# An attention and two-MLP kernel: v loaded in token order by five transfers, and loads planned by their size

## The chip, the cores and the metric

The kernel runs on one core of one Trainium2 chip. The metric is the device time of the kernel in microseconds (us); lower is better. The core has five engines with queues of their own: TensorE (PE) multiplies matrices, VectorE (DVE), ScalarE (ACT) and GpSimd (POOL) work on rows of data, and SyncE (SP) issues the transfers between device memory and on-chip memory. PEld is TensorE's loading of weights, which overlaps its matmuls.

## The reference

Three stages follow each other. Cut to what matters:

```python
def attn(q, k, v):                     # (4, 8, 576, 64) each: batch, head, token, dim
    q_lm = q.reshape(B, H, 32, 18, D).mean(axis=3)      # 32 landmarks of 18 tokens
    k_lm = k.reshape(B, H, 32, 18, D).mean(axis=3)
    A, Bm, C = sm(q, k_lm), sm(q_lm, k_lm), sm(q_lm, k) # softmax of scaled products
    Z = Bm.T / (norm1(Bm) * norminf(Bm) + 1e-6)
    for _ in range(6):
        Z = 2 * Z - Z @ Bm @ Z
    return A @ Z @ C @ v
x = attn(q, k, v) as (2304, 512)
xn = x / sqrt(mean(x * x) + 1e-6) * rms_g
x = (silu(xn @ w_gate) * (xn @ w_val)) @ w_out          # d_ff 1536
out = (s * relu(x @ w_in) ** 2 + b) @ w_out2            # d_ff 2048; s and b are scalars
```

The five weight matrices come as float64 and everything else too small to matter here; q, k and v are float32.

## The kernel before

The work runs in three stretches that overlap at their edges. First comes the attention of batch 0, which only one chain of small steps on DVE, ACT and PE can produce. Then comes the first MLP for batches 0 to 3, half a batch (288 tokens) at a time, in 48 units (a batch and one of 12 slices of d_ff); while it runs for batch b, the attention of batch b + 1 is worked in between. Last comes the second MLP, in five blocks of up to 512 tokens by 16 slices.

Weights are float64 in device memory. `narrow` loads a tile of 512 KB into a staging buffer (`stage`, three of them, and three more inside `xbuf` once the attention of batch 0 is done), and makes float32 of it with three passes on ACT (the lines that write `ca` and `cmag`; the third can go to DVE) and one on DVE (which writes `rawg` or `rawo`). In batch 0 each of 12 slices needs three such tiles (gate, val, out). `rawg` has three buffers of two tiles each. The float32 tiles are stored back to device memory (`keptg`, `kepto`), and later batches load them from there.

No loop fixes the order of instructions. Each piece of work is handed to a planner (`Scheduler`) as an operation with an engine, a cost in us, a key and the data that it reads and writes. The planner walks through a time of its own: it takes the engine that can start earliest, gives it the ready operation with the lowest key, and emits its instructions. So the costs decide the order in which each engine gets its instructions, and on the chip each engine keeps that order and waits wherever the data is late. For a transfer the cost is the time until its data is taken as landed, and SP counts as free again a fixed time before that:

```python
free[e] = end if e != "sp" else end - 2.0
...
at(("sp", 5.2 if fine else 3.9), -0.3 if b else 0, load_heads, w=[t])
...
op(("sp", 3.46), key - 12, load, w=[st])
```

Here `at` is how the attention of a batch hands over its work, `load_heads` loads one of q and k for half the heads (one transfer for batches 0 and 1, four for the `fine` batches 2 and 3), and `load` is that of a weight tile. Keys of an attention's operations follow from how much work hangs behind each (`by_path`); those of batch 0 lie between -60 and -6, and those of the first weight tiles near -20.

v of a batch is one buffer, token by partition: five groups of up to 128 tokens, each with eight heads of 64 numbers. Before, v is laid out by a token order in which tokens that are 18 apart stand beside each other, because the scores and their exponentials (`eC`) come out of TensorE in that order. That takes 18 transfers of 32 partitions each. The product of `eC` with v is `cv_mm`; it needs rows of both in one order.

Of the kernel before, what the change touches and what calls it, by code (L numbers as in the profile page):

```python
# [37 lines left out]
XC = 2.0  # L38
COLD1 = 6.5
GV = 8  # L40
W2_STEP = 4.2
TO_F, TO_R = 0.09, 0.11
HOLD, FETCH = 2.0, 4.0

# [46 lines left out]
class Scheduler:  # L91
# [67 lines left out]
    def run(self, warm):  # L159
        free = dict.fromkeys(self.engines, 0.0)  # L160
        cand = {e: [] for e in self.engines}
        for o in self.ops:
            if not o.n_deps:
                for e in o.alts:
                    cand[e].append(o)
        left = len(self.ops)
        mode = "f"
        steady = False
        while left:
            best, port = None, None  # L170
            for e, ops in cand.items():
                ready = [(t, o) for o in ops if (t := self.start_of(o, e)) is not None]
                if not ready:
                    continue
                at = max(free[e], min(t for t, _ in ready))
                if best is None or at < best[0]:
                    best = (at, e, ready)
                if e in ("dve", "pool"):
                    o = min((o for t, o in ready if t <= at + self.SOON), key=lambda o: o.key)
                    if e in o.pair and (port is None or o.key < port[3] and at < port[0] + self.WAIT):  # L180
                        port = (at, e, ready, o.key)
            if best[1] in ("dve", "pool") and port and port[1] != best[1] and port[0] < best[0] + self.WAIT:
                o = min((o for t, o in best[2] if t <= best[0] + self.SOON), key=lambda o: o.key)
                if best[1] in o.pair and port[3] < o.key:
                    best = port[:3]
            at, e, ready = best
            shift = {}
            if e == "pe" and steady:
                shift = {"f": HOLD if mode == "r" else -FETCH}
            can = sorted(((o.key + shift.get(o.mode, 0.0), t, o) for t, o in ready if t <= at + self.SOON), key=lambda x: x[:2])  # L190
            for _, t, o in can:
                end = max(at, t) + o.alts[e] + o.spare.get(e, 0.0)
                if all(
                    max(free[a], self.start_of(o, a)) + d + o.spare.get(a, 0.0) >= end
                    for a, d in o.alts.items() if a != e
                ):
                    break
            else:
                _, t, o = can[0]
                a = min(o.alts, key=lambda a: max(free[a], self.start_of(o, a)) + o.alts[a] + o.spare.get(a, 0.0))  # L200
                e, at = a, max(free[a], at)
                end = max(at, self.start_of(o, a)) + o.alts[a]
            if e == "pe":
                t = max(WARM0, free["pe"])
                while (t := t + WCOST * (2 if t < COLD1 else 1)) <= min(at, WARM1) - WARMS:
                    warm()
            at = max(at, self.start_of(o, e))
            if e == "pe" and o.mode:
                steady = steady or o.mode == "r"
                if steady and o.mode != mode:  # L210
                    at = max(at, free[e] + (TO_R if o.mode == "r" else TO_F))
                mode = o.mode
            end = at + o.alts[e] * (2 if e == "pe" and at < COLD1 else 1)
            for b, s in self.slots_for(o).items():
                b.slot = s
                s.held = True
                if b.ring.queue:
                    b.ring.queue.remove(b)
            o.fn(self.engines[e])
            free[e] = end if e != "sp" else end - 2.0  # L220
            if e in o.pair:
                self.ports = end
            for b in o.bufs:
                b.left -= 1
                b.end = max(b.end, end)
                if not b.left:
                    b.slot.held, b.slot.free = False, b.end
            for u in o.users:
                u.ready[e] = max(u.ready.get(e, 0.0), end)
                u.n_deps -= 1  # L230
                if not u.n_deps:
                    for a in u.alts:
                        cand[a].append(u)
            for a in o.alts:
                cand[a].remove(o)
            left -= 1
# [5 lines left out]

def t_dve2(n):
    return 0.07 + 0.00052 * n


def t_act(n):
# [16 lines left out]
def tile_nystrom_attention_two_mlps(  # L264
# [18 lines left out]
    M = 32  # L283
# [110 lines left out]
    def consts(_):  # L394
# [12 lines left out]
        out=ident, in_=ones, pattern=[[-1, 128]], compare_op=ALU.is_equal,  # L407
        fill=0.0, base=0, channel_multiplier=1), r=["const"], w=["ident"])

    def load_small(e):  # L410
        e.dma_start(out=gT, in_=rms_g.rearrange("(k p) -> p k", p=128))
        e.dma_start(out=s_sb, in_=s2.rearrange("(o k) -> o k", o=1).to_broadcast([128, 1]))
        e.dma_start(out=b_sb, in_=b2.rearrange("(o k) -> o k", o=1).to_broadcast([128, 1]))

    op(("sp", 3.3), -20, load_small, w=["small"]).after = 6.0


    xs, gw = {}, {}
# [7 lines left out]
    def attention(b, t0, t1):  # L426
# [41 lines left out]
        for nm, a in (("k", k), ("q", q)):  # L468
            for g in range(2):
                t = src[nm, g] = Buf(qk_r[nm, g])  # L470

                def load_heads(e, t=t, a=a, g=g):
                    if not fine:
                        e.dma_start(
                            out=t.t.rearrange("p (t d) -> p t d", d=D),
                            in_=a[b, 4 * g:4 * g + 4].rearrange("h (i t) d -> (h i) t d", t=SEG))
                        return
                    for h in range(4):
                        e.dma_start(
                            out=t.t[32 * h:32 * h + 32].rearrange("p (t d) -> p t d", d=D),  # L480
                            in_=a[b, 2 * h + g].rearrange("(i t) d -> i t d", t=SEG))

                at(("sp", 5.2 if fine else 3.9), -0.3 if b else 0, load_heads, w=[t])
        vs = Buf(v_r)

        def vt():
            return vs.t.rearrange("p (j h d) -> p j h d", j=5, h=H)

        def load_v(e):
            sv = v[b].rearrange("h (i n) d -> n i h d", n=SEG)  # L490
            for n in range(SEG):
                e.dma_start(out=vt()[32 * (n % 4):32 * (n % 4) + 32, n // 4], in_=sv[token(b, n)])

        at(("sp", 9.5), -0.25 if b else 0.01, load_v, w=[vs])


        def loaded(g, h):
# [201 lines left out]
        def c_side(g, p0):  # L699
# [5 lines left out]
            for hf in range(2):  # L705
# [3 lines left out]
                    out=cm.t[:, hf:hf + 1], in_=pC[hf].t[:, 0:HC], axis=AX, op=ALU.max),  # L709
                    r=[pC[hf]], w=[(cm, hf)])  # L710

            def c_max(e):
                e.tensor_reduce(out=cm.t[:, 2:3], in_=cm.t[:, 0:2], axis=AX, op=ALU.max)
                e.tensor_scalar(out=cm.t[:, 3:4], in0=cm.t[:, 2:3], scalar1=-scale, scalar2=None, op0=ALU.mult)
# [1 line left out]
            at(("dve", 0.32), p0 + 0.02, c_max, r=[(cm, 0), (cm, 1)], w=[(cm, 3)])  # L716
            for hf in range(2):
                at(("act", t_act(HC) + 0.19), p0 + 0.03, lambda e, hf=hf: e.activation(
                    out=eC.t[:, HC * hf:HC * hf + HC], in_=pC[hf].t[:, 0:HC], func=ACTF.Exp,
                    scale=scale, bias=cm.t[:, 3:4], accum_out=cs.t[:, hf:hf + 1]),  # L720
                    r=[pC[hf], (cm, 3)], w=[(eC, hf), (cs, hf)])

# [212 lines left out]
    def narrow(key, kind, f, part, dst, w, after=()):  # L935
# [22 lines left out]
            return x.rearrange("p (n t) -> p n t", t=2)[:, :, i]  # L958

        n_ops = len(S_.ops)  # L960
        op(("sp", 3.46), key - 12, load, w=[st])
        def low():
            x = staged().bitcast(U8)
            if rows:
# [23 lines left out]
    def first_weights(key, b, f):  # L988

        r = Buf(rg_r)  # L990
        if b == 0:
            for part in range(2):
                narrow(key + 2.6 * part, 1, f, part, lambda part=part: r.t[:, part], (r, part))
            kept[0, f] = dr.tile([128, 2, 512], F32, name=f"keptg{f}")
            op(("sp", 3.7), key + 9, lambda e: e.dma_start(out=kept[0, f], in_=r.t),
               r=[(r, 0), (r, 1)], w=[("kept", 0, f)])
        else:
            op(("sp", 3.7), key - 8, lambda e: e.dma_start(out=r.t, in_=kept[0, f]),
               r=[("kept", 0, f)], w=[(r, 0), (r, 1)])
        return r  # L1000

    def out_weights(key, b, hf, f):
        r = Buf(ro_r)
        if b == 0 and hf == 0:
            narrow(key, 1, f, 2, lambda: r.t, r)
            kept[1, f] = dr.tile([128, 512], F32, name=f"kepto{f}")
            op(("sp", 3.0), key + 6, lambda e: e.dma_start(out=kept[1, f], in_=r.t), r=[r], w=[("kept", 1, f)])
        else:
            op(("sp", 3.0), key - 8, lambda e: e.dma_start(out=r.t, in_=kept[1, f]), r=[("kept", 1, f)], w=[r])
        return r  # L1010

    def weights(key, ring, src, r):
# [132 lines left out]
    def second_mm(key, j, f, w, hs):  # L1145
# [15 lines left out]
        for c in range(nt):  # L1161
# [10 lines left out]
                        in_=o.t[32 * i:32 * i + 32, :])  # L1172

            if j < NB - 1:
                op(("sp", 4.2), key, lambda e, store=store: store(e, range(4)), r=[o])
                continue
            op(("sp", 3.1), key, lambda e, store=store: store(e, (0, 1)), r=[o])
            op(("act", 1.1), key, lambda e, store=store: store(e, (2, 3)), r=[o])

    LEAD, LEAD_O = 6, 5  # L1180
# [102 lines left out]
    for i in range(NB * F2):  # L1283
# [3 lines left out]
        if f == F2 - 4 and j + 1 < NB:  # L1287
# [12 lines left out]
            else e.tensor_tensor(out=r.t[:, 0:n], in0=r.t[:, 0:n], in1=r.t[:, 0:n], op=ALU.mult)), r=[r], w=[r])  # L1300
        op({"pool": 0.3 + 0.0018 * n, "dve": 0.18 + t_dve2(n)}, t, lambda e, r=r, h=h, n=n: e.tensor_scalar(
            out=h.t[:, 0:n], in0=r.t[:, 0:n], scalar1=s_sb, scalar2=b_sb, op0=ALU.mult, op1=ALU.add),
            r=[r, "small", "hidden"], w=[h], pair=True)
        hh, hl = Buf(hs_r[0]), Buf(hs_r[1])
        split(t + 3, lambda hh=hh, n=n: hh.t[:, 0:n], lambda hl=hl, n=n: hl.t[:, 0:n],
              lambda h=h, n=n: h.t[:, 0:n], [h], hh, hl, n)
# [47 lines left out]
```

## Time and profile before

| | |
|---|---|
| time, median of 3 runs | 874.73 us (874.48 to 875.18) |
| the profiled execution | 874.78 us, of which the span from first to last instruction is 873.1 us |
| PE, PEld, DVE, ACT, POOL busy | 97%, 82%, 78%, 54%, 14% of the span |
| moved by the DMA engines | 105.96 MB, 121 GB/s on the mean |
| mean granted TensorE clock | 0.993 of full speed |

The shares are means over stretches that are limited by different things, so they say little about one edit. Matmuls are pipelined and overlap in the record, so a busy PE is not a PE at its peak. The DMA share of a stretch is how busy the core's 16 DMA engines were on the mean; it can show slightly over 1.

### The profile page before, as it was taken

Reading aid. Unit: us, or ns where it says so; the run is one execution under the profiler, and the core shown is the slowest. Engines: PE = TensorE matmul, PEld = TensorE weight load, DVE = VectorE, ACT = ScalarE, POOL = GpSimd, SP = SyncE. Lnnn points to the kernel's source line nnn. Section 1 sums busy time; section 2 is a strip of 40 time slices with the busy share of each in tenths; the row PEclk is TensorE's granted clock in tenths of the full one; section 3 lists DMA queues with packets and bytes.
Section 4 is the critical chain, followed back from the end, with each engine's and each line's share of the span. In section 5 each row is a group of like instructions: output and inputs, shape, how many; then the busy total and the mean of one; then the engine's idle time right before and its main releaser. Section 6 shows DMA issues by size and latency. Waiting matters only on the chain.

```text
span 873.1 us, 16943 instructions
## 1 busy us (share of the span) xinstructions
PE 844.8 (97%) x6386; PEld 716.6 (82%) x6386; DVE 679.2 (78%) x1500; ACT 472.1 (54%) x961; POOL 119.7 (14%) x153
## 2 busy tenths in 40 slices
PE   8978999999999999999999999999999999999997
PEld 5666666998799988899999888888888888888896
DVE  6968787888899888999899766766676667666786
ACT  4869868455563355477997433433343334333453
POOL 0260035501870033201000000000000000000000
PEclk9989999999999999999999999999999999999999
DMA  7798897785535413478985000010000000000100
GB/s 223 214 342 274 294 301 222 230 253 169 140 114 177 127 69 97 132 234 272 307 264 169 1 1 1 22 27 1 1 24 25 1 1 25 23 1 1 37 13 24
DMA packets 72513, 105.96 MB, mean 121 GB/s; under 512 B 25584, under 2 KB 46064, under 8 KB 72432
## 3 DMA queue, kind: packets, MB, share of 16 engines
q1 hardware_dynamic: 72240, 104.62, 38.4%
q8 instruction: 50, 0.82, 0.4%
q10 hardware_dynamic: 192, 0.26, 0.1%
q14 instruction: 31, 0.25, 0.1%
HBM read 90.70 MB, written 14.16 MB: 120 GB/s over the span
## 4 chain that ended last, share of the span: by engine, by line
PE 76%; DVE 10%; ACT 5%; DMA 5%; issue 2%; POOL 1%; SPq 0%; DVEq 0%; ACTq 0%; POOLq 0%
PE bank L1033 23%; PE bank L1155 22%; PE bank L1129 12%; PE bank L1079 11%; PE bank L1052 2%; PE bank L676 1%; PE bank L556 1%; DMA region<-in_k_dram 1%; ACT ca L968 1%; DVE ul L1067 1%; ACT cmag L970 1%; DVE wl L931 1%; DMA kepto<-rawo 1%; PE bank L1317 1%; DVE hbuf L1098 1%
## 5 line engine op out<-in xcount | busy, mean ns | idle before, releaser
L1295 ACT ACTIVATE hbuf<-bank 128x512 f32<-128x512 f32 (+1 forms) x79 | 44.0, 557 | 144.4 <-PE bank L1033 144.0
L1033 PE MATMUL bank<-xh,ul 128*128 128x512 f32 (+1 forms) x320 | 117.7, 368 | 0.0
L1033 PE MATMUL bank<-xl,uh 128*128 128x512 f32 (+1 forms) x320 | 117.6, 368 | 0.0
L1033 PE MATMUL bank<-xh,uh 128*128 128x512 f32 (+1 forms) x320 | 117.6, 367 | 0.0
L1155 PE MATMUL bank<-wh,hh 128*128 128x512 f32 x288 | 112.4, 390 | 0.3 <-DVE hh L930 0.3
L1155 PE MATMUL bank<-wl,hh 128*128 128x512 f32 x288 | 112.3, 390 | 0.0
L1155 PE MATMUL bank<-wh,hl 128*128 128x512 f32 x288 | 112.0, 389 | 0.0
L1129 PE MATMUL bank<-hh,wh 128*128 128x288 f32 x336 | 102.4, 305 | 0.3 <-ACT xbuf L1139 0.3
L1129 PE MATMUL bank<-hh,wl 128*128 128x288 f32 x336 | 98.8, 294 | 0.0
L1129 PE MATMUL bank<-hl,wh 128*128 128x288 f32 x336 | 98.8, 294 | 0.0
L1079 PE MATMUL bank<-xh,uh 128*128 128x288 f32 x248 | 77.8, 314 | 6.1 <-DVE ul L1067 3.1
L931 DVE TENSOR_TENSOR hl<-hbuf,hh 128x512 fp32r<-128x512 f32 (+2 forms) x134 | 78.2, 584 | 3.3 <-ACT hh L929 0.9
L1079 PE MATMUL bank<-xh,ul 128*128 128x288 f32 x248 | 74.4, 300 | 1.1 <-DVE ul L1067 1.1
L1079 PE MATMUL bank<-xl,uh 128*128 128x288 f32 x248 | 74.1, 299 | 0.0
L1129 PEld LDWEIGHTS bank<-hh,wh 128*128 128x128 f32 x336 | 63.0, 188 | 10.2 <-issue 8.9
L1033 PEld LDWEIGHTS bank<-xh,uh 128*128 128x128 f32 x320 | 60.1, 188 | 11.2
L1033 PEld LDWEIGHTS bank<-xl,uh 128*128 128x128 f32 x320 | 60.1, 188 | 11.0
L1033 PEld LDWEIGHTS bank<-xh,ul 128*128 128x128 f32 x320 | 60.0, 188 | 10.1
L929 ACT ACTIVATE wh<-region 128x512 fp32r<-128x512 f32 x48 | 30.4, 633 | 67.1 <-PE bank L1155 67.1
L930 DVE CAST uh<-region 128x512 fp32r<-128x512 f32 x57 | 24.3, 426 | 54.2 <-PE bank L1033 54.2
L931 DVE TENSOR_TENSOR wl<-rawo,wh 128x512 fp32r<-128x512 f32 x79 | 60.1, 761 | 5.2 <-ACT wh L929 0.8
L1155 PEld LDWEIGHTS bank<-wh,hl 128*128 128x128 f32 x288 | 54.1, 188 | 11.5 <-DVE hl L931 0.2
(219 smaller groups left out, 1989.5 us busy)
## 6 DMA issues: line engine op xcount, KB each, us to landing
rawo<-kepto SPq DMA_DIRECT2D x84, 256.0 KB, 3.1
rawg<-keptg SPq DMA_DIRECT2D x36, 512.0 KB, 4.6
stage<-in_moe_w_out_dram SPq DMA_DIRECT2D x28, 512.0 KB, 4.7
stage<-in_moe_w_in_dram SPq DMA_DIRECT2D x16, 512.0 KB, 5.0
keptg<-rawg SPq DMA_DIRECT2D x12, 512.0 KB, 7.5
region<-in_v_dram SPq DMA_DIRECT2D x72, 64.0 KB, 2.7
stage<-in_moe_w_val_dram SPq DMA_DIRECT2D x8, 512.0 KB, 6.6
xbuf<-in_moe_w_gate_dram SPq DMA_DIRECT2D x7, 512.0 KB, 6.8
```

Source lines behind the costliest of these rows:

```text
L556: nc.tensor.transpose(pT.t[:, 128 * j:128 * j + 128], s3.t[:, c:c + 128], ident)
L676: nc.tensor.matmul(out=ps.t[:, 0:HC], lhsT=part(u, "bd")[:, 128 * e:128 * e + 128], rhs=part(y, "t").rearrange("p (t e i) -> p t e i", e=2 ...
L929: e.activation(out=hi(), in_=src(), func=ACTF.Copy) if e is nc.scalar
L930: else e.tensor_copy(out=hi(), in_=src())), r=r, w=[wh], pair=True)
L931: b = op({"dve": t_dve(n), "pool": t_pool(n)}, key, lambda e: e.tensor_tensor(out=lo(), in0=src(), in1=hi().bitcast(F32), op=ALU.subtract) ...
L968: op(("act", 0.08 + t_act(512)), key, lambda e: e.activation(out=wide(a.t), in_=word(1).bitcast(F32), func=ACTF.Copy, scale=2.0 ** -112), ...
L1033: nc.tensor.matmul(out=ps.t[:, 0:n], lhsT=w[a].t[:, ks], rhs=x[y].t[:, kd, 0:n], start=(kd == 0 and i == 0), stop=(kd == KD - 1 and i == 2))
L1052: nc.tensor.matmul(out=pU[g].t[m, 256 * j:256 * j + 256], lhsT=gw[b].t[p, m], rhs=r.t[p, :, 128 * k:128 * k + 128], start=True, stop=True)
L1079: nc.tensor.matmul(out=ps.t[:, 0:HC], lhsT=u[a].t[:, 256 * g + 128 * part:256 * g + 128 * part + 128], rhs=x[y].t.rearrange("p k n -> p (k ...
L1129: nc.tensor.matmul(out=A[c].t[:, 0:HC], lhsT=w[a].t[:, 128 * c:128 * c + 128], rhs=hs[y].t[:, 0:HC], start=(f == 0 and i == 0), stop=(f == ...
L1155: nc.tensor.matmul(out=A[c].t, lhsT=hs[a].t[:, s], rhs=w[y].t, start=(f == 0 and i == 0), stop=(f == F2 - 1 and i == 2))
L1295: e.activation(out=r.t[:, 0:n], in_=ps.t[:, 0:n], func=ACTF.Relu) if e is nc.scalar
```

## The change

Five edits are made together. (1) v is loaded in plain token order, by five transfers of up to 128 partitions (four of 256 KB and one of 128 KB) in place of 18 of 64 KB. (2) So that `eC` has the same order, the two exponential passes of a head group write their output through a rearranged view: each value goes 72 bytes from the one before it, where it went next to it. (3) The cost of a transfer is worked out from its size (`t_dma`), and SP is free 3.0 us before the data lands, not 2.0. (4) The RMS factor `gT` is loaded alone; (5) the scale and bias of the second MLP are loaded later, under a name of their own (`scale`). `V_SP` is not used.

```diff
+DMA_LAG = 3.0
+DMA_KB = 0.00272
...
-            free[e] = end if e != "sp" else end - 2.0
+            free[e] = end if e != "sp" else end - DMA_LAG
...
+def t_dma(kb, n=1):
+    return DMA_LAG + max(DMA_KB * kb, 0.45 * n)
...
+    op(("sp", t_dma(100)), -20, lambda e: e.dma_start(out=gT, in_=rms_g.rearrange("(k p) -> p k", p=128)),
+       w=["small"]).after = 6.0
+
     def load_small(e):
-        e.dma_start(out=gT, in_=rms_g.rearrange("(k p) -> p k", p=128))
         e.dma_start(out=s_sb, in_=s2.rearrange("(o k) -> o k", o=1).to_broadcast([128, 1]))
         e.dma_start(out=b_sb, in_=b2.rearrange("(o k) -> o k", o=1).to_broadcast([128, 1]))
 
-    op(("sp", 3.3), -20, load_small, w=["small"]).after = 6.0
+    op(("sp", t_dma(100, 2)), 200.0, load_small, w=["scale"]).after = 130.0
...
-                at(("sp", 5.2 if fine else 3.9), -0.3 if b else 0, load_heads, w=[t])
+                at(("sp", t_dma(600, 4 if fine else 1)), -0.3 if b else 0, load_heads, w=[t])
...
         def load_v(e):
-            sv = v[b].rearrange("h (i n) d -> n i h d", n=SEG)
-            for n in range(SEG):
-                e.dma_start(out=vt()[32 * (n % 4):32 * (n % 4) + 32, n // 4], in_=sv[token(b, n)])
-
-        at(("sp", 9.5), -0.25 if b else 0.01, load_v, w=[vs])
+            for j in range(5):
+                n = min(128, S - 128 * j)
+                e.dma_start(out=vt()[0:n, j], in_=v[b][:, 128 * j:128 * j + n].rearrange("h n d -> n h d"))
+
+        at(("sp", t_dma(1310, 5)), -0.25 if b else 0.01, load_v, w=[vs])
...
+            def in_order(hf):
+                x = eC.t[:, 0:S]
+                if fine:
+                    return x.rearrange("p (i n) -> p n i", i=M)[:, HB * hf:HB * hf + HB]
+                return x.rearrange("p (i t e) -> p e t i", i=M, e=2)[:, hf]
...
                 at(("act", t_act(HC) + 0.19), p0 + 0.03, lambda e, hf=hf: e.activation(
-                    out=eC.t[:, HC * hf:HC * hf + HC], in_=pC[hf].t[:, 0:HC], func=ACTF.Exp,
+                    out=in_order(hf), in_=pC[hf].t[:, 0:HC].rearrange("p (t i) -> p t i", i=M), func=ACTF.Exp,
...
-        op(("sp", 3.46), key - 12, load, w=[st])
+        op(("sp", t_dma(512)), key - 12, load, w=[st])
...
-            op(("sp", 3.7), key + 9, lambda e: e.dma_start(out=kept[0, f], in_=r.t),
+            op(("sp", t_dma(512)), key + 9, lambda e: e.dma_start(out=kept[0, f], in_=r.t),
...
-            op(("sp", 3.7), key - 8, lambda e: e.dma_start(out=r.t, in_=kept[0, f]),
+            op(("sp", t_dma(512)), key - 8, lambda e: e.dma_start(out=r.t, in_=kept[0, f]),
...
-            op(("sp", 3.0), key + 6, lambda e: e.dma_start(out=kept[1, f], in_=r.t), r=[r], w=[("kept", 1, f)])
+            op(("sp", t_dma(256)), key + 6, lambda e: e.dma_start(out=kept[1, f], in_=r.t), r=[r], w=[("kept", 1, f)])
         else:
-            op(("sp", 3.0), key - 8, lambda e: e.dma_start(out=r.t, in_=kept[1, f]), r=[("kept", 1, f)], w=[r])
+            op(("sp", t_dma(256)), key - 8, lambda e: e.dma_start(out=r.t, in_=kept[1, f]), r=[("kept", 1, f)], w=[r])
...
-                op(("sp", 4.2), key, lambda e, store=store: store(e, range(4)), r=[o])
+                op(("sp", t_dma(256, 4)), key, lambda e, store=store: store(e, range(4)), r=[o])
...
-            op(("sp", 3.1), key, lambda e, store=store: store(e, (0, 1)), r=[o])
+            op(("sp", t_dma(128, 2)), key, lambda e, store=store: store(e, (0, 1)), r=[o])
...
-            r=[r, "small", "hidden"], w=[h], pair=True)
+            r=[r, "scale", "hidden"], w=[h], pair=True)
```

## Rows read from the trace of the kernel before

**Rows 1.** Windows: busy us (instructions) by engine, clock, DMA share, GB/s.

```profile
0.00:8.00 8.00, 6.19 (x29) 4.34 (x30) 3.50 (x24) 2.95 (x5) 0.50 (x5) 1.00 0.75 271
...
10.00:16.00 6.00, 6.00 (x93) 4.13 (x91) 3.61 (x12) 3.74 (x10) 0.00 (x0) 1.00 0.59 120
...
36.00:44.00 8.00, 7.17 (x78) 5.18 (x79) 7.30 (x21) 7.14 (x17) 1.58 (x2) 1.00 0.46 92
44.00:60.00 16.00, 11.68 (x75) 9.42 (x73) 10.31 (x18) 9.45 (x21) 13.85 (x20) 0.79 0.98 329
60.00:150.00 90.00, 83.54 (x851) 60.31 (x849) 71.68 (x185) 76.06 (x154) 17.76 (x23) 1.00 0.87 284
150.00:482.00 332.00, 325.59 (x3154) 298.24 (x3154) 295.53 (x691) 203.34 (x446) 80.67 (x96) 1.00 0.58 182
482.00:860.00 378.00, 378.00 (x1750) 316.23 (x1749) 261.02 (x467) 150.85 (x267) 0.00 (x0) 1.00 0.05 12
```

**Rows 2.** Chain that ended last, in order of time: start us, us, what.

```profile
18.63 0.60 ACT region L718 x2
...
44.50 4.90 DMA stage<-in_moe_w_val_dram
...
54.16 2.96 PE bank L1079 x12
...
97.53 7.63 DMA kepto<-rawo
...
138.82 3.56 DMA rawg<-keptg
...
153.35 3.18 PE bank L1079 x24
```

**Rows 3.** Timeline of ACT, 16 to 50 us: start, us, instruction, idle before.

```profile
16.36 0.26 ACT L607 ACTIVATE region<-region 128x64 f32<-128x64 f32 x1 [1.83 <-DVE region L605]
18.63 0.50 ACT L718 ACTIVATE region<-bank,region 128x288 f32<-128x288 f32 x1 [1.46 <-DVE region L714]
...
21.21 0.67 ACT L968 ACTIVATE ca<-stage 128x512 f32<-128x512 f32 x1 [1.51 <-DMA stage<-in_moe_w_gate_dram]
...
36.24 0.78 ACT L978 ACTIVATE cmag<-stage 128x512 f16<-128x512 f32 x1
...
44.63 0.39 ACT L1096 ACTIVATE hbuf<-bank 128x288 f32<-128x288 f32 x1
49.42 0.67 ACT L968 ACTIVATE ca<-stage 128x512 f32<-128x512 f32 x1 [4.40 <-DMA stage<-in_moe_w_val_dram]
...
51.36 0.65 ACT L968 ACTIVATE ca<-stage 128x512 f32<-128x512 f32 x1
```

**Rows 4.** Timeline of SP's transfers, 0 to 60 us: start, us, issue, count.

```profile
2.77 13.24 SPq L492 DMA_DIRECT2D region<-in_v_dram  x18
16.06 1.11 SPq L951 DMA_DIRECT2D stage<-in_moe_w_gate_dram  x1
...
19.31 0.51 SPq L411 DMA_DIRECT2D gT<-in_moe_rms_g_dram  x1
...
29.14 15.27 SPq L492 DMA_DIRECT2D region<-in_v_dram  x18
44.50 0.40 SPq L951 DMA_DIRECT2D stage<-in_moe_w_val_dram  x1
```

**Rows 5.** Single lines: issues of v, narrowing's third and second pass, and L842.

```profile
L492 SPq DMA_DIRECT2D region<-in_v_dram x72: 311/449/1496, 2.8 to 229.1; - x72
...
L978 ACT ACTIVATE cmag<-stage x54: 767/792/811, 22.5 to 470.7; 128x512 f16<-128x512 f32 x54
...
L970 ACT ACTIVATE cmag<-stage x57: 643/667/727, 21.8 to 470.0; 128x512 int32<-128x512 uint8 x57
...
L842 DVE TENSOR_TENSOR gw<-bank,gT x4: 281/288/293, 37.2 to 355.5; 128x128 f32<-128x128 f32 x4
```

**Rows 6.** SP's own waits, 0 to 60 us: total us, times, longest.

```profile
SPq L492 <- DMA region<-in_q_dram: 6.8, 4, 2.1
```

More of the change, by code (lines that the diff above doesn't have):

```diff
@@ L40 @@
 GV = 8
+V_SP = 5.0
 W2_STEP = 4.2
+DMA_LAG = 3.0
+DMA_KB = 0.00272
 TO_F, TO_R = 0.09, 0.11
```

## The prediction

> **What bounds the kernel now.** I read the table of windows first, to see which stretch can give time. From 482 to 860 us PE is busy in every microsecond and the transfers stand nearly still, and from 150 to 482 us PE lacks only 6.4 us of 332 [rows 1]: nothing about loads is to be won there, and a shift of what comes before is passed on whole. Between 60 and 150 us ACT is busy 76.1 of 90 us and the DMA engines 87%: float64 weights are loaded and narrowed there, and the two share the limit. The soft place is earlier. From 36 to 44 us the DMA engines are 46% busy at 92 GB/s, from 10 to 16 us 59% at 120 GB/s, although the stretches after each are short of weights [rows 1].
>
> The timeline of SP says why. v of batch 0 takes SP from 2.77 to 16.01 us, 18 issues, and the first weight tile is issued at 16.06. v of batch 1 takes it from 29.14 to 44.41, and the next weight tile (`w_val`, the sixth) is issued at 44.50 [rows 4]. SP does one thing at a time, so whatever stands behind v waits; part of it is that v's issues wait themselves for older transfers to land (6.8 us behind loads of q, in four waits) [rows 6].
>
> The timeline of ACT says what that costs. It is done at 45.02 (44.63 + 0.39) and starts the sixth tile at 49.42, 4.40 us idle until that load has landed [rows 3]. The chain of waits runs through the same load: 4.90 us from 44.50, then the narrowing, then 12 matmuls at 54.16 [rows 2]. The other chain links ahead of 44 us are attention of batch 0, on DVE, ACT and PE in turn, not loads; after 150 us they are matmuls.
>
> **The change, part by part.**
>
> *v by five transfers.* An issue of v takes 0.31 to 1.50 us, 0.45 in the middle [rows 5]. The trace has none of 256 KB with eight short runs per partition; five of them take SP 1.6 us if each costs the least and 7.5 if each costs the most. I take 2.7, five times 0.45 and one issue more for the gaps between them. Second train: 29.14 + 7.5 = 36.6 even at the dear end. The staging buffer that the sixth tile needs is the third tile's, whose last pass ends at 36.24 + 0.78 = 37.02 [rows 3]. So at either end of the bounds SP is free before the buffer is; the load goes out at about 37.0 and lands at about 37.0 + 4.9 = 41.9 [rows 2], before ACT is done with its attention work at 45.02. The whole wait goes: **-4.4 us**. What is late next is ACT itself: the sixth tile can also be narrowed in the gaps before 45. A tile occupies it 51.36 - 49.42 = 1.94 us [rows 3]. The three `rawg` buffers hold six tiles, so no more than this one gains: 0 to 1.94, and I take half, **-1.0**.
>
> First train: on the chip it should end near 5.5 us instead of 16.0 and free SP some 10 us earlier, but v's bytes must still pass. From 10 to 16 us the DMA engines moved 120 GB/s at a share of 0.59 [rows 1], so 203 GB/s at a full one; 1.18 MB of v take 5.8 us, behind q and k, of whose 2.36 MB 2.17 are through at 8 us (271 GB/s); the tile's own 0.52 MB take 1.6 us at the 329 GB/s of 44 to 60 us. So it lands at about 8.7 + 5.8 + 1.6, 16 to 17 us, where it was waited for until 21.21 [rows 3]. Up to 44 us the attention chain decides, so this alone gives nothing; it is what makes room for the sixth tile above. Later trains free SP too, but under a busy PE: nothing.
>
> *PE after the gap.* The 12 matmuls at 54.16 take 2.96 us [rows 2], 24 of the same kind take 3.18 at 153.35, so 1.59 for 12: the granted clock is 0.79 on the mean from 44 to 60 us [rows 1], between the levels 2.4 and 1.2 GHz, and PE is busy for only 11.7 of those 16 us. With the idle shorter, 0 to 1.37 us come back; half of it, **-0.7**.
>
> *Exponentials with a step of 72 bytes.* 16 passes of 288 columns; in batch 0 two at a time stand in the chain (0.60 us for two starting at 18.63) [rows 2], one takes 0.50 [rows 3]. No row shows ACT storing at such a step. From below: nothing, since reads and short steps cost little: the third narrowing pass stores two bytes in every four at 0.79 us, the second stores whole words at 0.67 [rows 5]. From above: every pass twice as long, 0.5 more for each of the two in the chain, 1.0. I take a value near the lower end, since the nearest row is there: those two passes differ by 18%, which is 0.2 on the two, and a little more for the longer step: **+0.3**. The Trainium skill (SBUF — State Buffer, in the section on the DMA port swizzle) speaks against this edit: on-chip memory has lines of 16 bytes, and every access that crosses into a new one pays, so that only four float32 words can be stepped over freely; 72 bytes crosses one each time. The page gives no factor; with the doubling the sum below would be 0.7 us higher, and no run here shows which holds.
>
> *The costs in the plan.* SP's slot is the cost less 2.0 before, less 3.0 after: a coarse q or k load 1.9 becomes 1.63, v 7.5 becomes 3.56 (1310 x 0.00272), a weight tile 1.46 becomes 1.39; the tile counts as landed 4.39 us after its slot begins and not 3.46. The first tile was expected at 4 x 1.9 + 7.5 + 3.46 = 18.6 and came at 21.2; now it is expected at 4 x 1.63 + 3.56 + 4.39 = 14.5. Everything that follows is dealt anew, on all engines. I cost that at nothing on the mean, with a bound either way of one load more or less in the chain: links there take 3.56 to 7.63 us [rows 2], and I keep the smaller.
>
> *`gT`, scale and bias.* `gT` is issued at 19.31 [rows 4] and first used at 37.2 [rows 5]; two issues fewer before it change nothing. Scale and bias are read only after 482 us, and their two issues (0.5 us each) fall into a stretch where PE has its work: nothing. Without that cover it would be 1 us.
>
> **Sum.** -4.4 - 1.0 - 0.7 + 0.3 = -5.8, from the profiled execution's own 874.78 (its span of 873.1 and 1.7 around it): **869.0 us**. The median of the runs is 874.73, so the forecast is the same against it.
>
> **The rivals.**
>
> *Given back before 150 us.* The 5 us are won at 45, but 60 to 150 us runs at a DMA share of 0.87 with ACT at 85%, and batch 1's attention must also be finished by 150. If that attention and not the weights sets the end, or if the transfers have no more to give, all but about 1 us is lost: 873.8. For it: both shares. Against it: the chain in 44 to 60 us is weights, and the share of 0.46 ahead of it is idle transfer time of 4 us that gets used.
>
> *ACT stuck behind an early tile (slower).* The plan now puts the first tile's passes into ACT's order at about 14.5 us, ahead of attention passes that ran at 16.36 (L607) and 18.63 (L718) [rows 3]. ACT can't step over them. If five large transfers drain no faster than 18 small ones, the tile still lands at 21.2, L718 starts after its first pass, at 21.9 rather than 18.6, 3.3 us late in the very chain that sets the end; the second train then holds SP as before too, and nothing is won: 878.1. It decides from a landing after 18.6 on. For it: a plan that expects 14.5 where I work out 16 to 17. Against: 5.8 us of bytes.
>
> *A new wait from the new deal.* A load that the planner now thinks quick (`fine` q and k 1.8 us of SP instead of 3.2) goes ahead of a kept tile, and PE waits once for 3.56 us: 869.0 + 3.6 = 872.6. The opposite, one link of 97.53 or 138.82 gone as well: 865.4.
>
> **How the numbers follow.** The likeliest case has a range of its own from 874.78 - 4.4 - 1.94 - 1.37 = 867.1 to 874.78 - 4.4 + 1.0 = 871.4, chance 0.45. One link fewer (862 to 867) 0.15, one more (871.4 to 873) 0.11, given back (873 to 876.5) 0.12, slower 0.17. The range 863 to 877 leaves out the best part of the gains and about half of the slower case, 0.18 together. About 0.2%, 1.75 us, is what a measurement can tell from no change: faster 0.71, same 0.12, slower 0.17.
>
> **What would show it.** Right: v as five issues of under 1.5 us; SP at work on `w_val` by 38 us; ACT's wait of 4.4 us before 50 gone; the DMA share of 36 to 44 us well above 0.46; the second MLP starting some 5 to 6 us earlier and lasting as long. Wrong: exponentials of 0.7 us and more; ACT idle for a load before 20 us; the start of the second MLP unmoved although the wait at 45 is gone (given back); a PE idle of over 2 us between 100 and 482 us that was not there.

## The result and the profile after

The changed kernel takes 881.00 us, median of four runs (878.27 to 881.65), beside 874.61 for the kernel before (four runs, 874.26 to 875.18): ratio 1.0067, 95% interval 1.0044 to 1.0089. It is slower by some 6 us; the forecast was 5.8 us faster. The profiled execution took 881.65, its span 880.0. In the changed kernel v is issued at L501 (L492 before), a weights tile at L966 (L951), narrowed at L983, L985 and L993 (L968, L970, L978), the Exp is L733 (L718), the MLP's first products are L1067 and L1094 (L1052, L1079).

The windows of the changed kernel, in the columns of [rows 1], with some stretches of my choice:

```profile
0.00:8.00 8.00, 6.65 (x35) 4.85 (x36) 3.55 (x24) 3.31 (x7) 0.50 (x5) 1.00 0.75 277
10.00:16.00 6.00, 4.08 (x79) 2.91 (x77) 4.33 (x19) 2.55 (x8) 0.67 (x1) 1.00 1.19 244
16.00:36.00 20.00, 15.65 (x286) 8.94 (x288) 14.05 (x59) 11.47 (x26) 4.70 (x7) 0.68 0.90 275
36.00:44.00 8.00, 7.07 (x65) 4.62 (x62) 5.84 (x15) 6.88 (x17) 0.00 (x0) 0.94 0.39 135
44.00:60.00 16.00, 12.01 (x107) 9.67 (x107) 14.48 (x30) 14.53 (x30) 12.52 (x15) 1.00 0.94 313
60.00:150.00 90.00, 82.81 (x842) 58.86 (x841) 69.33 (x171) 75.82 (x157) 24.06 (x35) 0.96 0.93 298
150.00:482.00 332.00, 324.20 (x3143) 297.02 (x3143) 292.31 (x704) 195.19 (x430) 64.42 (x83) 1.00 0.56 175
482.00:860.00 378.00, 378.00 (x1749) 316.41 (x1748) 261.37 (x469) 148.32 (x260) 0.00 (x0) 1.00 0.05 12
```

The stretch from 10 to 16 us has what was hoped for: a DMA share of 1.19 and 244 GB/s where [rows 1] have 0.59 and 120. ACT is busy 14.5 us of 44 to 60 and no longer 9.5. But 36 to 44 us stays at a share of 0.39, and the granted clock, 1.00 from 60 to 150 us in [rows 1], is 0.96 there and 0.68 from 16 to 36. From 150 us on nothing differs but a shift: the first product of the second MLP (L1048, L1033 before) starts at 463.97 us instead of 456.78, and the last ends as much later.

SP's transfers in the changed kernel, beside [rows 4]:

```profile
2.72 8.70 SPq L501 DMA_DIRECT2D region<-in_v_dram  x5
11.46 0.72 SPq L966 DMA_DIRECT2D stage<-in_moe_w_gate_dram  x1
...
29.13 5.05 SPq L501 DMA_DIRECT2D region<-in_v_dram  x5
37.04 0.35 SPq L1010 DMA_DIRECT2D keptg<-rawg  x1
41.09 0.37 SPq L966 DMA_DIRECT2D stage<-in_moe_w_val_dram  x1
```

SP gets to the first tile 4.6 us earlier and is done with the second v at 34.2, ten us earlier. `w_val`, forecast for 37.0, goes out at 41.09 all the same.

ACT, 14 to 24 us, beside [rows 3], then ACT at 40 us:

```profile
14.61 0.26 ACT L616 ACTIVATE region<-region 128x64 f32<-128x64 f32 x1 [1.84 <-DVE region L614]
16.44 0.69 ACT L983 ACTIVATE ca<-stage 128x512 f32<-128x512 f32 x1 [1.57 <-DMA stage<-in_moe_w_gate_dram]
17.04 0.43 ACT L806 ACTIVATE region<-region 128x288 f32<-128x288 f32 x1
17.37 0.64 ACT L985 ACTIVATE cmag<-stage 128x512 int32<-128x512 uint8 x1
18.04 0.78 ACT L993 ACTIVATE cmag<-stage 128x512 f16<-128x512 f32 x1
18.69 0.77 ACT L733 ACTIVATE region<-bank,region 128x288 f32<-128x288 f32 x1
...
40.29 0.78 ACT L993 ACTIVATE cmag<-stage 128x512 f16<-128x512 f32 x1
```

DVE just ahead of that Exp (its input is the result of L729), and what DVE waits for afterwards:

```profile
16.62 0.15 DVE L729 TENSOR_SCALAR region<-region 128x1 f32<-128x1 f32 x1
...
22.59 0.29 DVE L668 SCALAR_TENSOR_TENSOR region<-region,bank 128x128 f32<-128x128 f32 x1 [3.12 <-ACT cmag L993]
...
86.41 0.45 DVE L1117 SCALAR_TENSOR_TENSOR xbuf<-hbuf,bank 128x288 f32<-128x288 f32 x1 [2.29 <-DMA xbuf<-in_moe_w_val_dram]
...
96.93 0.45 DVE L1117 SCALAR_TENSOR_TENSOR xbuf<-hbuf,bank 128x288 f32<-128x288 f32 x1 [2.74 <-DMA xbuf<-in_moe_w_gate_dram]
```

PE behind that Exp:

```profile
19.52 1.18 PE L698 MATMUL bank<-xbuf,region 64*32 64x288 f32 x8 [2.00 <-ACT region L733]
...
21.81 0.65 PE L623 MATMUL bank<-region 32*32 32x64 f32 x16
...
28.75 0.43 PE L772 MATMUL bank<-region 128*32 128x64 f32 x16
30.69 1.02 PE L772 MATMUL bank<-region 128*32 128x64 f32 x24 [1.51 <-issue]
...
34.95 3.21 PE L876 MATMUL bank<-region 64*128 64x288 f32 x16
...
42.07 0.66 PE L1067 MATMUL bank<-rawg,gw 64*32 64x256 f32 x16
```

The same rows in the kernel before (L757 for L772, L861 for L876, L1052 for L1067):

```profile
28.24 0.90 PE L757 MATMUL bank<-region 128*32 128x64 f32 x40
...
31.79 2.26 PE L861 MATMUL bank<-region 64*128 64x288 f32 x16
...
38.03 0.66 PE L1052 MATMUL bank<-rawg,gw 64*32 64x256 f32 x16
```

**The first loss:** attention of batch 0 is 1.75 us ahead of the kernel before (L616 at 14.61, L607 at 16.36), and the Exp's last input is there at 16.77 (16.62 + 0.15). But the planner has put the three passes over the first weights tile ahead of it in ACT's list; the tile lands at 16.4, ACT idles 1.57 us for it, and the Exp starts at 18.69, 1.9 us after it could. PE waits 2.00 us for it and gets to its next product of the chain (L623) at 21.81, so DVE has nothing that it can do for 3.12 us before 22.59 (its row names a pass of ACT, but that is over at 21.98 and L623 at 22.46). That takes the lead away and 0.5 us more: the row of 40 products L772 starts at 28.75 us, the same row (L757) in the kernel before at 28.24. By the first product of the MLP the lateness is 4 us (42.07 instead of 38.03), and 3.5 of these come after 28.75: PE stops for 1.51 us in the middle of that row, then has the clock at 0.50 from 30.18 to 37.01 us, where the 16 products of L876 take 3.21 us and not 2.26. The stop goes with the early tile: it is 0.79 to 1.51 us long in this kernel and the three below that have the tile ahead of the Exp, and 0.32 us at most in all others. The last section says what else the traces show of it.

**The second loss:** L1117 writes blocks of the hidden layer into the end of each row of `xbuf`; `st_late`, three staging buffers for weights, lies in strips across all four rows of `xbuf`, so a strip's address range takes in the hidden blocks of rows 0 to 2, though not one word is shared. DVE waits twice for a load into such a strip, 2.29 and 2.74 us.

Behind the early tile and behind each of the two waits TensorE idles and is then granted the lower clock, as windows around those places show:

```profile
12.00:16.53 4.53, 2.70 (x88) 1.78 (x92) 3.07 (x12) 0.84 (x4) 0.67 (x1) 1.00 1.13 270
16.53:23.35 6.82, 4.82 (x49) 1.65 (x36) 3.39 (x19) 5.50 (x12) 0.00 (x0) 0.50 1.06 363
...
84.00:88.21 4.21, 2.56 (x28) 1.45 (x28) 1.92 (x5) 2.08 (x7) 0.00 (x0) 1.00 1.02 398
88.21:91.62 3.41, 3.41 (x38) 1.67 (x36) 0.91 (x3) 1.96 (x5) 0.00 (x0) 0.50 0.96 322
95.00:98.45 3.45, 1.86 (x20) 0.65 (x19) 1.52 (x4) 2.79 (x6) 0.00 (x0) 1.00 1.09 306
98.45:101.86 3.41, 3.41 (x9) 1.94 (x7) 1.90 (x6) 2.52 (x7) 0.00 (x0) 0.50 1.02 354
```

PE was busy 2.70 of 4.53, 2.56 of 4.21 and 1.86 of 3.45 us before the clock fell to 0.50, its 1.2 GHz level.

### The profile page after: what moved, and what is told of

It is laid out like the page before. It is cut to its first block, busy times and chain, and to the rows that moved or that the text cites. A ratio compares the mean times of both kernels' runs of the same rounds, so it can differ in the third digit from the quotient of the medians.

```text
span 880.0 us, 16939 instructions
## 1 busy us (share of the span) xinstructions
PE 847.6 (96%) x6405; PEld 717.7 (82%) x6405; DVE 680.3 (77%) x1514; ACT 467.1 (53%) x952; POOL 106.9 (12%) x144
## 4 chain that ended last, share of the span: by engine, by line
PE 81%; DVE 8%; ACT 4%; DMA 3%; issue 2%; SPq 1%; DVEq 0%; ACTq 0%
PE bank L1048 22%; PE bank L1170 22%; PE bank L1144 12%; PE bank L1094 12%; PE bank L1067 2%; PE bank L1140 2%; DMA stage<-in_moe_w_in_dram 2%; PE bank L685 1%; PE bank L623 1%; PE bank L1332 1%; PE bank L876 1%; SPq L501 1%; DVE rawg L997 1%; DVE hbuf L1113 1%; ACT ca L983 1%
## 5 line engine op out<-in xcount | busy, mean ns | idle before, releaser
L1048 PE MATMUL bank<-xh,ul 128*128 128x512 f32 (+1 forms) x320 | 117.7, 368 | 0.0
L1048 PE MATMUL bank<-xl,uh 128*128 128x512 f32 (+1 forms) x320 | 117.7, 368 | 0.0
L1048 PE MATMUL bank<-xh,uh 128*128 128x512 f32 (+1 forms) x320 | 117.6, 368 | 0.0
L1094 PE MATMUL bank<-xh,uh 128*128 128x288 f32 x248 | 77.2, 311 | 4.6 <-DVE ul L1082 3.0
L1094 PE MATMUL bank<-xl,uh 128*128 128x288 f32 x248 | 73.1, 295 | 0.0
L1094 PE MATMUL bank<-xh,ul 128*128 128x288 f32 x248 | 73.1, 295 | 0.0
L1048 PEld LDWEIGHTS bank<-xh,uh 128*128 128x128 f32 x320 | 60.2, 188 | 11.3
L1048 PEld LDWEIGHTS bank<-xl,uh 128*128 128x128 f32 x320 | 60.1, 188 | 10.9
L1048 PEld LDWEIGHTS bank<-xh,ul 128*128 128x128 f32 x320 | 60.1, 188 | 10.0
L1144 PEld LDWEIGHTS bank<-hl,wh 128*128 128x128 f32 x336 | 63.1, 188 | 0.3
```

Of the source, the lines that this page charges most:

```text
L1048: nc.tensor.matmul(out=ps.t[:, 0:n], lhsT=w[a].t[:, ks], rhs=x[y].t[:, kd, 0:n], start=(kd == 0 and i == 0), stop=(kd == KD - 1 and i == 2))
L1094: nc.tensor.matmul(out=ps.t[:, 0:HC], lhsT=u[a].t[:, 256 * g + 128 * part:256 * g + 128 * part + 128], rhs=x[y].t.rearrange("p k n -> p (k ...
L1144: nc.tensor.matmul(out=A[c].t[:, 0:HC], lhsT=w[a].t[:, 128 * c:128 * c + 128], rhs=hs[y].t[:, 0:HC], start=(f == 0 and i == 0), stop=(f == ...
```

## The experiments

Every time is compared with the kernel before on the same chip. Theory 1: the loads are as good as forecast, and the newly priced plan loses more, at the two places above. The rivals: the denser bursts of v, or the stepped Exp, do the harm.

**The loads and the Exp without the new plan.** The kernel before with two edits of the change:

```
-            for n in range(SEG):
-                e.dma_start(out=vt()[32 * (n % 4):32 * (n % 4) + 32, n // 4], in_=sv[token(b, n)])
+            for j in range(5):
+                n = min(128, S - 128 * j)
+                e.dma_start(out=vt()[0:n, j], in_=v[b][:, 128 * j:128 * j + n].rearrange("h n d -> n h d"))
...
+                    out=in_order(hf), in_=pC[hf].t[:, 0:HC].rearrange("p (t i) -> p t i", i=M), func=ACTF.Exp,
```

> The kernel before, its plan and every cost untouched, with two edits of the change alone: v in token order by five transfers, and the exponentials stored with the 72-byte step. Theory 1 (the new deal of the plan loses the time: the first weight tile's passes stand ahead of the exponentials on ACT, and hidden writes wait for loads): the old order keeps both away, SP is free early, so ACT's wait of 4.4 us before 50 us goes and the longer exponentials (0.79 for 0.49 us, two pairs in the chain) cost 0.6 to 1.2 us: about 871 us. Theory 2 (the burst of five large transfers itself holds up what is loaded behind it): near the changed kernel, 879 to 881 us.

873.38 us beside 876.15, ratio 0.9962 (0.9935 to 0.9990), as theory 1 has it. Its trace has what the forecast described:

```profile
36.00:44.00 8.00, 6.15 (x66) 4.25 (x65) 7.49 (x18) 7.21 (x17) 3.52 (x4) 1.00 0.84 226
44.00:60.00 16.00, 13.14 (x116) 10.94 (x117) 12.96 (x27) 13.80 (x30) 12.39 (x18) 1.00 1.02 366
```

The DMA share of 36 to 44 us is 0.84 and not 0.46 [rows 1]; `w_val` goes out at 35.44. So five transfers, with the stepped Exp, are worth some 3 us, and the bursts are not what loses.

**The step of the Exp alone**: the Exp as above, 18 transfers in token order, the old plan:

```
+                e.dma_start(out=vt()[32 * (n % 4):32 * (n % 4) + 32, n // 4],
+                            in_=v[b][:, 32 * n:32 * n + 32].rearrange("h n d -> n h d"))
```

> The kernel before with its plan, v in token order but still by 18 transfers of 32 partitions, and the exponentials stored with the 72-byte step. Theory 1: only the exponentials' 0.3 us each, two pairs of them in the chain of batch 0: 0.6 to 1.2 us over before, about 875.6 us. Theory 3 (the longer exponentials are what costs the changed kernel its time, through idle PE and its clock): 879 to 881 us.

876.71 us, ratio 1.0007 (0.9990 to 1.0023): 0.6 us, not told from nothing; the Exp is not the 6 us.

**The new plan alone**, with the 18 old transfers and the old Exp (the inverse of the diff above, made in the changed kernel):

> The changed kernel's plan and order, with v by 18 transfers in the old token order and the exponentials stored side by side as before. Theory 1: the plan alone is worse than the whole change, since 18 transfers keep SP until 16 us, the first tile lands near 21 us and the exponentials stand behind it on ACT: about 883 us. Theory 2 (the burst) and theory 3 (the exponentials) both expect the time of before, 874 to 876 us.

888.01 us, ratio 1.0145 (1.0117 to 1.0172): more than theory 1 had worked out, in its direction. ACT waits there as the slower rival of the prediction had it:

```profile
20.35 0.66 ACT L983 ACTIVATE ca<-stage 128x512 f32<-128x512 f32 x1 [5.56 <-DMA stage<-in_moe_w_gate_dram]
...
22.57 0.47 ACT L733 ACTIVATE region<-bank,region 128x288 f32<-128x288 f32 x1
```

**The second loss alone.** The changed kernel with the late weights staged inside one row of `xbuf`, clear of the hidden blocks; the order of instructions stays:

```
-    st_late = [Slot(far[:, :, 256 * i:256 * i + 256].bitcast(I64)) for i in range(3)]
+    st_late = [Slot(xbuf[:, i, S:S + 1024].bitcast(I64)) for i in range(3)]
```

> The changed kernel with the three late staging buffers in other columns of the same tile (rows of 4 KB in one piece, so that the addresses from the first to the last of a buffer hold no slot of a hidden block); order and costs are unchanged on every engine. Theory 1: the two waits of hidden writes (L1117) for loads into xbuf, 2.29 and 2.74 us, go, and with them some of the half clock after them: 5 to 6.7 us off, 874 to 876 us. Theories 2 and 3: nothing to do with it, 880 to 881 us.

877.47 us, ratio 1.0012 (0.9993 to 1.0031). L1117 waits for no load any more, and 0.0055, 4.8 us, come back: a little less than expected.

**Which part of the plan.** First the split of the small loads on the old plan with five loads:

```
+    op(("sp", 3.3), -20, lambda e: e.dma_start(out=gT, in_=rms_g.rearrange("(k p) -> p k", p=128)),
+       w=["small"]).after = 6.0
...
-    op(("sp", 3.3), -20, load_small, w=["small"]).after = 6.0
+    op(("sp", 3.3), 200.0, load_small, w=["scale"]).after = 130.0
```

> The kernel before with the five transfers of v, the Exp that stores in order, and the split of the small loads: the RMS factor alone early, scale and bias after 130 us; the planner keeps its old prices and its lag of 2.0. Theory 1 (what the change loses comes from the new prices): it stands where the five loads alone stand, ratio to the kernel before about 0.996 (some 871 us beside 874.6), since the first weights tile stays behind the first Exp on ACT. Rival (the split is what turns the plan, since one early transfer instead of three lets SP reach the weights sooner): the first weights tile comes ahead of the first Exp, and the time is 878 to 882.

874.31 us, ratio 0.9996 (0.9976 to 1.0015). Neither prediction: 3 us above the kernel without the split, though the intervals overlap, and the first tile stays behind the Exp. The last run below comes back to it. Then the changed kernel with the small loads together again, so that loads, Exp and prices are left:

```
+        e.dma_start(out=gT, in_=rms_g.rearrange("(k p) -> p k", p=128))
...
-    op(("sp", t_dma(100, 2)), 200.0, load_small, w=["scale"]).after = 130.0
+    op(("sp", t_dma(100, 3)), -20, load_small, w=["small"]).after = 6.0
```

> The changed kernel with the three small loads together again, early; everything else of the change stays: five transfers, the Exp in order, the new prices and the lag of 3.0. Theory 1 (the new prices do the harm): ratio about 1.006, 879 to 881 us beside 874.6, with the first weights tile on ACT ahead of the first Exp and DVE waiting for a weights load inside xbuf between 84 and 100 us. Rival (the split does the harm): about 0.996, 871 us.

880.91 us, ratio 1.0079 (1.0056 to 1.0101), with the tile at 16.39 and the first Exp at 18.63 on ACT. The prices, with the lag of 3.0 us that belongs to them, do it: 1.0079 - 0.9962 = 0.0117, about 10 us against the same loads under the old prices.

**The first loss alone.** The changed kernel with the first two tiles' work held back in the plan:

```
-            o.after = RELC
+            o.after = 17.0 if key < 10 else RELC
```

> The changed kernel, but the first pair of weights tiles is held until 17 us in the plan, so that ACT's list has the first two Exp ahead of the tile's three operations, as the kernel before has; PE's and DVE's lists are the same as in the changed kernel, and on SP the last two transfers of the first heads go one place earlier. Theory 1 (the tile in front of the first Exp is worth the 1.9 us that the Exp waited, and the half-speed stretch of TensorE behind it): first Exp at about 16.8 us, the first product of the MLP 2 to 4 us earlier than in the changed kernel, and by 150 us about 2 us of it is left: ratio 1.002 to 1.005, 876.5 to 879 us. Rival (the loss up to 38 us is the denser transfers of v and the stall of TensorE at 29 us): the first Exp comes earlier, the MLP starts as late as in the changed kernel, ratio 1.006 to 1.008.

877.98 us, ratio 1.0026 (1.0007 to 1.0045). The Exp starts when its input is there, and the MLP's first product at 37.54 us instead of 42.07. PE has the same list of instructions as in the changed kernel, but its stop is 0.18 us and not 1.51, and its clock is 1.00 from 30 to 44 us. But the second loss grows to one wait of 6 us:

```profile
16.81 0.80 ACT L733 ACTIVATE region<-bank,region 128x288 f32<-128x288 f32 x1 [1.46 <-DVE region L729]
```

```profile
93.76 0.46 DVE L1117 SCALAR_TENSOR_TENSOR xbuf<-hbuf,bank 128x288 f32<-128x288 f32 x1 [6.01 <-DMA xbuf<-in_moe_w_gate_dram]
```

Theory 1 holds: 4.5 us are won by 38 us, of which the Exp itself is 1.9, and 3.6 are left in the ratio.

**Loads apart on the old plan**, the `st_late` edit made in the first experiment's kernel:

> The kernel before with the five transfers and the Exp that stores in order, its old plan and prices, and the late weights staged in a place of their own that the hidden blocks do not share; the order of all instructions is that of the same kernel without the last edit. Theory 1 (hidden blocks wait for loads that merely lie between their addresses): the 4.0 us wait of DVE behind the store of an output tile is not touched, but the lead of 6 us that this kernel has at 84 us is given back less: ratio 0.992 to 0.995, 868 to 870 us. Rival (the lead is given back at the store of the output tile and in the clock, not at the staging): ratio about 0.996, 871 us.

870.20 us, ratio 0.9956 (0.9935 to 0.9977) beside 0.9962 without the edit. Here the rival is right: under the old plan that staging costs nothing that can be measured. There too, without the edit, DVE waits once for a load into such a strip, but only 1.2 us (0.9 in the kernel before). How long the wait is depends on how the order of instructions brings a load and a hidden block together.

**Both repairs**, `after = 17.0` and `st_late`, in the changed kernel:

> The changed kernel with both repairs: the first pair of weights tiles held until 17 us in the plan, and the late weights staged apart from the hidden blocks. Alone the first gave ratio 1.0026 and the second 1.0012, where the changed kernel has 1.0067. Theory 1 (two separate losses, which add): 1.0067 - 0.0041 - 0.0055 = 0.997, some 872 us beside 874.6, and in the trace no wait of DVE for a weights load between 84 and 100 us. Rival (one loss, met at two places; the store of the output tiles and the clock take what either gains): 1.001 to 1.003, 875.5 to 877 us.

874.26 us, ratio 0.9989 (0.9969 to 1.0008). Of the 0.0096 that the two would give if they added, 0.0078 came. The full sum (0.9971) lies inside the interval and the rival's 1.001 just outside; no L1117 waits for a load any more, and the first product of the second MLP starts at 455.68 us. So two losses fit better than one met twice, though over the second repair alone (1.0012) the first adds only 0.0023, and these two intervals overlap.

**The price of v as measured.** The changed kernel with `st_late` and one number mended:

```
-        at(("sp", t_dma(1310, 5)), -0.25 if b else 0.01, load_v, w=[vs])
+        at(("sp", DMA_LAG + 8.5), -0.25 if b else 0.01, load_v, w=[vs])
```

> The changed kernel with the staging apart and one price mended: the five transfers of v at 8.5 us plus the lag, as SP's list shows them (8.70 us of SP from 2.72 in the changed kernel, 8.44 in the old plan), where the change has 3.56 plus the lag. The plan then puts both first Exp ahead of the first weights tile on ACT by itself. Theory 1 (this one price is what moved the tile): first Exp at about 16.8 us, first product of the MLP at 37 to 39 us, ratio 0.995 to 0.999, 870.5 to 874 us. Rival (the other new prices do as much harm): the first Exp early all the same, but 876 to 880 us.

875.54 us, ratio 0.9987 (0.9958 to 1.0016), with no order forced: the planner itself puts the Exp first (16.89 us), and the MLP starts at 37.59. One price, 3.56 us for what takes SP 8.70, moved the tile. In time this kernel is not told apart from the one with `st_late` alone (1.0012), nor from the kernel before (median 874.48 us there).

**The Exp in another order.** The loops of the stepped Exp turned round, in the kernel of old plan, five loads and loads apart (below, the form of batches 2 and 3, the `fine` ones, whose rows are nine words; batches 0 and 1 store every second word):

```
-                    return x.rearrange("p (i n) -> p n i", i=M)[:, HB * hf:HB * hf + HB]
+                    return x.rearrange("p (i n) -> p i n", i=M)[:, :, HB * hf:HB * hf + HB]
...
-                    out=in_order(hf), in_=pC[hf].t[:, 0:HC].rearrange("p (t i) -> p t i", i=M), func=ACTF.Exp,
+                    out=in_order(hf), in_=pC[hf].t[:, 0:HC].rearrange("p (t i) -> p i t", i=M), func=ACTF.Exp,
```

> The old plan with five loads and the staging apart, as run before (ratio 0.9956, 870.2 us), but each Exp goes over its tile in the order of the store: nine (or, in three batches, every second) neighbouring elements to a row, and the step is in the read of PSUM instead. Theory 1 (the step of 72 bytes in the store is what made 0.49 us into 0.79): 0.49 to 0.60 us each, and 1 to 2 us less in all, ratio 0.993 to 0.995. Rival (any stepped side costs the same): 0.75 to 0.85 us each and ratio 0.995 to 0.996. What the three batches with a step of 8 bytes take tells how far it goes with the step.

869.63 us, ratio 0.9929 (0.9905 to 0.9954), the fastest of all. The single line of the Exp, in the changed kernel and then here:

```profile
L733 ACT ACTIVATE region<-bank,region x14: 772/792/802, 18.7 to 323.3; 128x288 f32<-128x288 f32 x14
```

```profile
L724 ACT ACTIVATE region<-bank,region x14: 502/515/519, 17.5 to 313.3; 128x288 f32<-128x288 f32 x14
```

0.79 us becomes 0.515, where the plain store took 0.49: theory 1 in the single pass. What it does for the whole, 0.0027, is of the expected size, but the intervals overlap.

**The split once more**, on that fastest kernel:

> The fastest kernel so far (old plan, five loads, staging apart, Exp by rows; ratio 0.9929, 869.63 us) with one part of the change more, the split of the small loads as run before on the old plan (there 0.9996 beside 0.9962 without it, intervals that overlap). Theory 1 (the split costs some 3 us, since the plan deals other work after it): ratio 0.995 to 0.998, 870.5 to 873 us. Rival (the split costs nothing and the difference was the spread of the runs): 0.992 to 0.994, 868 to 869.5 us.

871.41 us, ratio 0.9939 (0.9915 to 0.9964) beside 0.9929. The split costs 0.9 us or nothing here; in both pairs the intervals overlap, so the 3 us seen before can be spread.

## Why the prediction was wrong

*v by five transfers.* Right in kind, wrong in size for SP. I took 2.7 us of SP for five and 7.5 as the dear end; the first train took 8.70, with single issues of 2.04 and 3.91 us, the second 5.05. The landing of the first tile was right (16 to 17 us worked out, 16.4 read). Alone the loads and the Exp gave 3 us, not 5.8.

*The sixth tile.* "SP is free before the buffer is" held: SP was free at 34.2. The buffer was not: the third tile's last pass, at 37.02 in [rows 3], ended at 41.07 (40.29 + 0.78), and `w_val` left at 41.09. The 4.40 us of [rows 3] are gone, and the same 4 us had been lost ahead of it.

*The costs in the plan, "at nothing on the mean", one load either way.* This step failed. The new prices cost some 10 us, beyond the bound of one load (3.56 us). A cost that moves an instruction to another place in an engine's fixed list is no small term with two signs: a tile expected at 14.5 us that lands at 16.4 holds whatever stands behind it.

*"ACT stuck behind an early tile".* That rival came, with its mechanism and a wrong point of decision. I let it decide from a landing after 18.6 us, when the Exp ran in [rows 3]. But the same change brought attention forward, and the Exp was ready at 16.77; its three passes ahead take 2.1 us (0.69 + 0.64 + 0.78), so any landing after some 14.7 us delayed it. With that point my own 16 to 17 us made this rival the likeliest case. Two of the signs that I had named for being wrong came: ACT idle for a load before 20 us, and Exp passes of over 0.7 us.

*What no step had.* The hidden blocks' waits for weights loads (4.8 us), PE's stop of 1.51 us at 29 us, and the lower clock behind some of the gaps: up to 860 us the changed kernel's profile has 20.5 us at 0.50 (6.8 from 16.5 and from 30.2 us, 3.4 from 88.2 and from 98.5), that of the kernel before 10.2. I had looked for the clock only in the gap that the change was to close, and there it did go to 1.00 (44 to 60 us).

*The Exp.* Each pass takes 0.30 us more, between the bounds of 0 and 0.5; the +0.3 of the sum had counted half of that for each of its two passes. By the rule of the Trainium skill (SBUF — State Buffer, in the section on the DMA port swizzle) every access into a new 16-byte line pays; the passes agree: 0.79 us at a step of 72 bytes, 0.515 at 8 bytes or in runs of nine words, 0.49 without a step.

*The small loads* cost little or nothing that can be measured, as forecast. Open remains what else the new prices cost: with both losses mended the changed kernel stands at 0.9989, the same loads under the old plan at 0.9962, and the intervals overlap.

## What to carry to other kernels

When a planner's costs are changed, cost the first instruction that changes its place in each engine's list, and compare the landing of what it waits for with the time at which the instruction behind it is ready in the new kernel, not in the old one. A price for a group of transfers has to include what the queue makes the issuing engine wait, not only bytes over bandwidth: here 8.7 us stood where 3.6 were charged. Buffers laid in strips across another buffer's rows waited for each other here without sharing a word, and how long can change with any edit to the order of work (1.2 us in one plan, 6 in another).

## What the runs showed of the hardware

- An Exp pass of ACT over 288 float32 words per partition takes 0.49 us when it stores them in a row, 0.515 us at a step of 8 bytes or in runs of 36 bytes, 0.79 us at 72 bytes. The 0.515 include reading PSUM at a step of 128 bytes, which so costs 0.03 us at most.
- In the changed kernel PE stood still for 1.51 us in the middle of a row of small products (L772, 29.18 to 30.69 us), waiting for nothing that the profile shows. Nine of the fourteen kernels stop in that row, always after its 16th product (after the 13th with the new plan alone), for 0.1 to 1.5 us. In all nine, PE goes on 1.24 to 1.44 us after a block of 16 KB has landed on queue 8, which the profile calls "instruction" (here at 29.25 us). In the five that don't stop, that block had landed over 1.7 us before the 17th product. So PE seems to wait for the next block of its own instructions; no run tested this, and why the block comes later in some kernels is open. The issue of v, which begins at 29.13 us here, does not do it: in the last two kernels above the stop is over before v is issued (28.92 and 29.12 us, 27.53 and 27.89 us).
- One program's time spreads along with its clock: ten executions of the kernel with the measured price lie between 869.51 us at a mean granted clock of 0.996 and 879.44 us at 0.988. Differences of 2 us need many runs here.
